# A fused retention and feed-forward kernel: one sum cut in halves, one block prepared earlier, some stores and transposes exchanged

## The chip, the cores and the metric

The kernel runs on one core of one Trainium2 chip. The metric is the device time of one execution in microseconds. Before the change it is 295.54 us, the median of three runs (295.34 to 296.19).

## The reference

Eight batches and eight heads of retention (attention without a softmax, with a decay per head), then two matrix products with `h * cos(h)` between them. All in float32.

```python
def _attn_ref(q, k, v):                       # each (8, 8, 576, 64)
    scores = scale * np.matmul(q, k.transpose(0, 1, 3, 2))      # scale = 1/8
    gamma = 1.0 - 2.0 ** (-5.0 - np.arange(H, dtype=np.float32))
    rel = pos[:, None] - pos[None, :]
    Dmat = np.where(rel >= 0, gamma[:, None, None] ** rel[None, :, :], 0.0)
    return np.matmul(scores * Dmat[None], v)

def _moe_ref(x, w_in, w_out):                 # (4608, 512), (512, 2048), (2048, 512)
    h = x @ w_in
    g = h * np.cos(h)
    return g @ w_out

x = attn_out.transpose(0, 2, 1, 3).reshape(8 * 576, 512)
out = _moe_ref(x, w_in, w_out)                # (4608, 512)
```

## The kernel before

**Tokens.** The 4608 tokens are cut into 18 blocks of 256 (the retention's unit) and 9 tiles of 512 (the two products' unit); tile n holds blocks 2n and 2n+1. The decay is split into a factor on q and one on k, so that a block's retention is: scores of the block with itself under a 0/1 mask, plus q against a state carried from the blocks before, which is a running sum of k times v.

**A block's steps, by function.** `load(j)` brings fq, fk, fv from DRAM, on SP's queue. `scaled` multiplies q or k by its factors and rounds to bf16 (`qks`); `prep(j)` does all four halves of a block on GpSimd. `round_v` rounds v to bf16 (`vb`). The product q·k needs both with the head dimension on partitions: `transpose_dma(j)` does that for a whole block with one transposing transfer on SP's queue (L197, tile `qkT`), `transpose_pe` with eight TensorE instructions and a copy out of PSUM (L210, L215). Blocks 0 to 3 use TensorE, all later ones the transfer. `scores` multiplies (L244 or L282) and puts the mask on with VectorE (`ret`, L262 or L292). `sums_of` multiplies k and v for the state (L319) and adds it to the running one (L349). `out_own` and `out_carried` are the block's two output products (L375, L407), and ScalarE copies the result into `xT`, the first layer's input.

**A tile's steps.** The first layer, `mm1`, works in eight pieces of 1024 columns per partition: TensorE (L445), the cosine on ScalarE (L457), the product with h on VectorE (L460), which writes the bf16 `gT`. The pieces go in turn through the PSUM banks a, b and m. The second layer of tile 0 is a plain product (L927). From tile 1 on, it is done with seven half-size products instead of eight (`mm2_seven`, L563): gT and w_out are cut into quarters, and the products take sums of quarters. The sums of w_out (`ws`) are made once. Those of gT, `gs5`, `gs6`, `gs7` and `gs3`, are made for each tile by `g_sum` (L503): three on VectorE, and one on GpSimd, in four pieces of 128x512. In tile 1 GpSimd makes sum 3, in later tiles sum 7. In tile 1 the products run in the order 1, 2, 4, 6, 5, 7, 3 and in later ones 1, 2, 6, 4, 7, 5, 3. ScalarE copies some products out of PSUM (L593), VectorE adds others to them (L589), and `stored_rows` stores each result in two transfers (L579). The four quarters of a tile's result are c11, c21, c22 and u1; `op` has two buffers for each of the names a, b, c and d.

**What sets the order.** The order on every engine is written by hand; an engine works through its list and waits where a semaphore says so. `at` in the last loop puts the retention of coming blocks between the seven products: `first_scores`, `next_scores` and `last_outputs` in tile 1; `only_intro`, `mid_unit` and `end_unit` in tile 2; `first_unit` and `second_unit` in later ones. `pend` collects the adds and stores of finished products, and `flush` issues them. `sums_after` puts sums behind certain pieces of the first layer, `late_sums` the rest behind the last. `step` is one block's `prep`, `transpose_dma`, `round_v` and the load of a later block; `steps_to` calls it until a block is prepared, and `stored(u)` calls that behind a store. SP's queue carries loads, transposes and stores in one order; the weights come over GpSimd's queue, and some of the last stores over ScalarE's.

**The places of the diff.** At the start, block 1's k has its second transpose on TensorE, and VectorE copies it out (L215) ahead of scaling block 1's q (L167). In tile 1, GpSimd's sum 3 stands between VectorE's sums 6 and 7 in `first_scores` and depends on sum 6 alone; tile 0's stores go out behind the first piece of the first layer, ahead of block 5's transpose; block 7 is prepared behind the store of c22. In tile 2, block 8 is prepared behind the seventh piece of the first layer, and half of VectorE's sum 3 is made behind the sixth. In the last tile, product 5 has three parts, of 256, 128 and 128 columns, for two row halves (the second is cut), of which the two smaller ones share the PSUM tile m; product 3 is accumulated on top of it.

Of the kernel before, what the change touches and what calls it, by code (L numbers as in the profile page):

```python
# [8 lines left out]
F32 = mybir.dt.float32  # L9
# [8 lines left out]
def kernel(  # L18
# [9 lines left out]
    nc = tc.nc  # L28
    P = 128
# [12 lines left out]
    E2 = ET // 2  # L42
# [160 lines left out]
    def transpose_pe(j, name, bank, evac, ys=(0, 1)):  # L203
        if ("qkT", j) not in tiles:
            new_qkT(j)
        m = "qk".index(name)
        ps = psum.tile([P, len(ys), HG, P], BF16, tag=bank, name="tr")
        for u, y in enumerate(ys):
            for hg in range(HG):
                nc.tensor.transpose(  # L210
                    ps[:, u, hg, :],
                    tiles["qks", j][:, m, y, hg].rearrange("s a d -> s (a d)"),
                    ident,
                )
        evac(tiles["qkT", j][:, m, ys[0] : ys[-1] + 1], ps)  # L215
# [298 lines left out]
    def sums_after(n, i):  # L514
        if n == 1:
            slots = {5: ((5, 0, 4),), 6: ((6, 0, 4),)}
        else:
            slots = {
                2: ((7, 0, 4),),
                3: ((5, 0, 4),),  # L520
                4: ((6, 0, 4), (7, 4, 6)),
                5: ((3, 0, 4),),
                6: ((5, 4, 6), (7, 6, E2)),
            }
        for x in slots.get(i, ()):
            g_sum(n, *x)

    def late_sums(n, xs):
        for x in xs:
            g_sum(n, x, 6 if x == 5 and n > 1 else 4, E2)  # L530

    def product(n, x, halfway=None):
        gT = tiles["g", n]
        parts = [(j, 0, N2) for j in range(2)]
        fold = n in (1, last)
        fresh = x not in ((6, 7, 3) if fold else (6, 7))
        if fresh:
            tag = {1: "n", 2: "st", 4: "m" if n == 1 else "st", 5: "st", 3: "n"}[x]
            if x == 5 and n == last:
                ps = psum.tile([P, N2], F32, tag="b", name="o")  # L540
                pt = psum.tile([P, 2, 512], F32, tag="m", name="o")
                tiles["o", x] = [ps] + [pt[:, k, : N2 // 2] for k in range(2)]
            else:
                ps = psum.tile([P, 2, N2], F32, tag=tag, name="o")
                tiles["o", x] = [ps[:, j] for j in range(2)]
                tiles["all", x] = ps
        if x in (5, 3) and n == last:
            parts = [(0, 0, N2), (1, 0, N2 // 2), (1, N2 // 2, N2)]
        dst = tiles["o", x if fresh else 5 if x == 3 else 1]
        lhs = {1: gT[:, :E2, :256], 2: gT[:, E2:, :256], 4: gT[:, E2:, 256:]}.get(x)  # L550
        if lhs is None:
            lhs = tiles["gs", n, x]
        rhs = {1: w_quarter(0, 0), 2: w_quarter(1, 0), 3: w_quarter(1, 1)}.get(x)
        if rhs is None:
            rhs = w_sum[x]
        order = [(e, i) for e in range(E2) for i in range(len(parts))]
        if len(parts) > 2:
            order.sort(key=lambda u: u[1])
        for u, (e, i) in enumerate(order):
            if halfway and u == len(order) // 2:  # L560
                halfway()
            j, c0, c1 = parts[i]
            nc.tensor.matmul(  # L563
                dst[i],
                lhsT=lhs[:, e, j * P : (j + 1) * P],
                rhs=rhs[:, e, c0:c1],
                start=(fresh and e == 0 and (i == 0 or len(parts) > 2)),
                stop=(e == E2 - 1 and (i == len(parts) - 1 or len(parts) > 2)),
                skip_group_check=True,
            )  # L570
        return parts

    def stored_rows(r0, c0, c1, t, queues=(nc.sync, nc.sync)):

        rows = out[r0 : r0 + P * t.shape[1], c0:c1].rearrange(
            "(j i r) c -> r i j c", r=2, i=HP
        )
        for r in range(2):
            queues[r].dma_start(rows[r], t[r * HP : (r + 1) * HP])  # L579

    def mm2_seven(n, at, stored, xs=(1, 2, 6, 4, 7, 5, 3), halfway=None):
# [13 lines left out]

        def store(t, r, c, s):
            def go():
                queues = (nc.sync, nc.scalar) if n == last and s == 2 else (nc.sync, nc.sync)
                stored_rows(n * W + r * 256, c * N2, (c + 1) * N2, t, queues)
                stored(s)  # L600

            return go
# [62 lines left out]
    def load_next(**kw):  # L665
        nonlocal loaded
        if loaded < NB:
            load(loaded, **kw)
            loaded += 1
# [116 lines left out]
    load_next(names="kqv", gate=w_dma[3])  # L786
    ps0 = psum.tile([P, DG, BK], F32, tag="m", name="ov")
    out_own(0, ps0)
    transpose_pe(1, "k", "st", vec, (1,))
    scaled(nc.vector, 1, "q", 0)  # L790
    scaled(nc.vector, 1, "q", 1)
    out_carried(0, ps0)
    act(x_of(0), ps0)
    nc.scalar.activation(sine, half_pi, ACTF.Sin, bias=0.0, scale=1.0)
# [70 lines left out]
    for n in range(NT):  # L865
        blocks = blocks_of.get(n) or [(e + k * E2, 0, W) for e in range(0, E2, 2) for k in range(2)]
        for i, (et, c0, cw) in enumerate(blocks):
            inside = {
                (0, 1): {2: block1_carried},
                (1, 0): {2: lambda: transpose_pe(3, "q", "b", act)},  # L870
                (1, 2): {3: block3_scores},
                (1, 3): {2: lambda: sums_of(3, "st")()()},
            }.get((n, i), {})
            off = [] if (n, i) == (1, 3) else None
            between = block1_sums if (n, i) == (0, 0) else None
            mm1(n, et, c0, cw, banks_of.get(n, "abmabmab")[i], inside, off, between)
            if (n, i) == (0, 0):
                block1_own()
            if (n, i) == (1, 0):
                step(False)  # L880
                load_next()
                for r0, ot in stores:
                    stored_rows(r0, 0, DM, ot)
            if (n, i) == (1, 1):
                step(False)
                load_next()
                step()
            if (n, i) == (1, 3):
                mm2_seven(1, {}, None, (1,), lambda: (outputs(3, "m"), off.pop()()))
            if n:  # L890
                sums_after(n, i)
            if (n, i) == (2, 6):
                step()
        if n == 0:
            gT = tiles["g", n]
            two = psum.tile([P, 2, DM], F32, tag="m", name="o")
# [67 lines left out]

        def first_scores(flush, pend):
            g_sum(n, 5, 4, E2)
            g_sum(n, 6, 4, E2)
            masks = scores(a, "ab")
            add_a = sums_of(a, "st")
            add_b = sums_of(b, "m")  # L970
            masks[0]()
            add_a()()
            masks[1]()
            g_sum(n, 3, 0, E2)
            g_sum(n, 7, 0, 4)
            tiles["rounded"] = add_b()
            g_sum(n, 7, 4, E2)

        def next_scores(flush, pend):
            outputs(a, "a")  # L980
# [30 lines left out]

        def stored(u):
            if n == 1:
                steps_to({2: 8}.get(u, 0))
            else:
                steps_to({0: 2 * n + 6, 3: 2 * n + 7}.get(u, 0))

# [31 lines left out]
```

## Time and profile before

| what | us |
|---|---|
| median of three runs | 295.54 |
| the profiled execution | 296.28 |
| its span, first to last instruction | 294.6 |
| TensorE's matmuls, busy | 283.2 |
| VectorE, busy | 215.6 |
| GpSimd, busy | 145.6 |
| ScalarE, busy | 143.0 |
| tile 1's stage, 51.7 to 86.6: TensorE busy | 33.77 of 34.90 |
| tile 2's stage, 86.6 to 117.5: TensorE busy | 30.57 of 30.90 |
| tile 4's stage, 147.0 to 176.5: TensorE busy | 29.39 of 29.50 |
| the last stage, 264.0 to 294.6: TensorE busy | 25.94 of 30.60 |
| mean granted TensorE clock | 0.994 |

The profiled execution is one execution; its time is compared with its own span, and only then with the median. TensorE's weight loads run beside its matmuls. A busy share says nothing about the order of things: which wait decides is read from the chain of waits and the timelines. Times in a timeline are counted from the span's start. The 16 transfer engines are taken up almost completely until some 215 us (their row over 40 slices shows 9 in all but a few slices), and much less after that.

### The profile page before, as it was taken

To read this page: it belongs to the slowest core of one execution; us is meant where nothing else is said; L and a number is where in the kernel's file an instruction comes from. 1 tells how busy PE (TensorE), PEld (TensorE's weight loads), DVE (VectorE), ACT (ScalarE), POOL (GpSimd) and SP (SyncE) were. 2 spreads that over 40 slices of the span, in tenths; PEclk is the share of its full clock that TensorE was granted. 3 is DMA by queue.
4 is the path that set the end of the run, shared out by engine and by line. 5 is a ranking of instruction groups with operands and counts; after the bars stand their busy time and mean duration, and the time that the engine had idled before them with its cause. 6 is when DMAs were issued, how large, how long until landed. Compare 5 with 4: busy or idle time off the path is not lost.

```text
span 294.6 us, 7623 instructions
## 1 busy us (share of the span) xinstructions
PE 283.2 (96%) x3248; PEld 195.0 (66%) x3268; DVE 215.6 (73%) x268; ACT 143.0 (49%) x166; POOL 145.6 (49%) x172
## 2 busy tenths in 40 slices
PE   7889999999999999999999999999999999999993
PEld 2568755878864688458845884588458845874583
DVE  4585748558986999699659965996599659835933
ACT  4466537646436624563356335633563356326620
POOL 8641535847864495839713961497148014102400
PEclk9799999999999999999999999999999999999999
DMA  7999999999899999999999999979930630121014
GB/s 197 268 222 215 232 247 214 231 181 231 198 199 227 204 240 210 191 219 197 236 203 193 243 215 197 219 128 223 203 64 21 127 71 0 38 65 44 2 37 107
DMA packets 128930, 49.78 MB, mean 169 GB/s; under 512 B 89344, under 2 KB 128384, under 8 KB 128896
## 3 DMA queue, kind: packets, MB, share of 16 engines
q1 hardware_dynamic: 124288, 44.84, 75.6%
q0 software_dynamic: 4224, 4.19, 8.8%
q8 instruction: 25, 0.41, 0.6%
q10 hardware_dynamic: 384, 0.26, 0.4%
q14 instruction: 9, 0.07, 0.1%
HBM read 36.70 MB, written 9.44 MB: 157 GB/s over the span
## 4 chain that ended last, share of the span: by engine, by line
PE 79%; DVE 10%; DMA 4%; POOL 2%; ACT 2%; issue 1%; DVEq 0%; ACTq 0%
PE h L445 38%; PE o L563 27%; PE o L927 5%; DVE gT L460 3%; PE ov L375 3%; DVE gs L503 3%; DMA qkT<-qks 2%; PE st L319 2%; POOL qks L167 2%; PE sc L282 2%; DVE ret L292 2%; PE ov L407 1%; DMA fk<-in_k_dram 1%; PE tr L210 1%; ACT cosh L457 1%
## 5 line engine op out<-in xcount | busy, mean ns | idle before, releaser
L445 PE MATMUL h<-xT,w_in_sb 128*128 128x512 bf16 (+1 forms) x690 | 126.6, 340 | 1.0
L460 DVE TENSOR_TENSOR gT<-h,cosh 128x1024 bf16<-128x1024 f32 x72 | 87.9, 1221 | 37.5 <-ACT cosh L457 37.4
L457 ACT ACTIVATE cosh<-h,half_pi 128x1024 f32<-128x1024 f32 x72 | 80.2, 1114 | 66.4 <-PE h L445 65.1
L445 PEld LDWEIGHTS <-w_in_sb 128*128 128x128 bf16 x704 | 68.4, 98 | 55.3 <-issue 0.6
L503 POOL TENSOR_TENSOR gs<-gT 128x512 bf16<-128x512 bf16 x28 | 35.8, 1280 | 92.2 <-DVE gT L460 92.2
L563 PEld LDWEIGHTS <-gs 128*128 128x128 bf16 x528 | 49.5, 98 | 6.4
L167 POOL TENSOR_TENSOR qks<-fq,gq 128x512 bf16<-128x512 f32 x31 | 33.9, 1113 | 18.1 <-DMA fq<-in_q_dram 14.9
L563 PEld LDWEIGHTS <-gT 128*128 128x128 bf16 x384 | 37.1, 98 | 6.3
L593 ACT COPY ot<-o 128x512 f32<-128x512 f32 x33 | 19.3, 586 | 40.5 <-PE o L563 40.5
L167 POOL TENSOR_TENSOR qks<-fk,gkc 128x512 bf16<-128x512 f32 x28 | 31.8, 1154 | 0.0
L589 DVE TENSOR_TENSOR ot<-ot,o 128x512 f32<-128x512 f32 x35 | 23.2, 680 | 10.9 <-ACT ot L593 7.9
L563 PE MATMUL o<-w_out_sb,gs 128*128 128x256 bf16 (+1 forms) x264 | 30.6, 269 | 0.0
L563 PE MATMUL o<-ws,gs 128*128 128x256 bf16 (+1 forms) x264 | 30.5, 270 | 0.0
L563 PE MATMUL o<-w_out_sb,gT 128*128 128x256 bf16 x256 | 30.5, 273 | 0.0
L292 DVE TENSOR_TENSOR ret<-sc,mask_c 128x1024 bf16<-128x1024 f32 x25 | 29.7, 1214 | 0.1
L430 ACT CAST xT<-ov 128x1024 bf16<-128x1024 f32 x16 | 16.2, 1013 | 11.0 <-PE ov L407 11.0
L178 POOL CAST vb<-fv 128x512 bf16<-128x512 f32 x31 | 18.7, 624 | 5.7 <-DMA fv<-in_v_dram 5.6
L503 DVE TENSOR_TENSOR gs<-gs,gT 128x1024 bf16<-128x1024 bf16 x16 | 15.7, 982 | 0.3
L503 DVE TENSOR_TENSOR gs<-gT 128x512 bf16<-128x512 bf16 (+1 forms) x25 | 15.4, 615 | 0.4
L563 PE MATMUL o<-ws,gT 128*128 128x256 bf16 x128 | 15.3, 273 | 0.0
L349 DVE TENSOR_TENSOR s<-st,s 128x256 f32<-128x256 f32 x18 | 7.6, 421 | 10.4 <-PE st L319 10.1
L359 ACT CAST sb<-s 128x512 bf16<-128x512 f32 (+1 forms) x18 | 10.3, 573 | 9.3 <-DVE s L347 3.8
(81 smaller groups left out, 203.4 us busy)
## 6 DMA issues: line engine op xcount, KB each, us to landing
out_dram<-ot SPq DMA_DIRECT2D x69, 128.0 KB, 2.6
fk<-in_k_dram SPq DMA_DIRECT2D x25, 256.0 KB, 5.7
fv<-in_v_dram SPq DMA_DIRECT2D x25, 256.0 KB, 5.1
fq<-in_q_dram SPq DMA_DIRECT2D x12, 512.0 KB, 5.3
w_in_sb<-in_moe_w_in_dram POOLq DMA_DIRECT2D x4, 512.0 KB, 8.1
w_out_sb<-in_moe_w_out_dram POOLq DMA_DIRECT2D x4, 512.0 KB, 9.8
fk<-in_k_dram SPq DMA_DIRECT2D x3, 512.0 KB, 5.3
fv<-in_v_dram SPq DMA_DIRECT2D x3, 512.0 KB, 7.0
```

The lines of the kernel that those rows point to most:

```text
L167: return eng.tensor_tensor(out=dst.rearrange("p b a d -> p a b d"), in0=src.rearrange("p (a b) d -> p a b d", a=2), in1=by.rearrange("p (a ...
L178: runs[y](vb[:, y], f[:, :, y, :] if j < NP_B else f[:, y])
L292: nc.vector.tensor_tensor(out=ret[:, k].rearrange("p a b i -> p (a b) i"), in0=pss[k].rearrange("p a b i -> p (a b) i"), in1=mask.unsqueez ...
L430: evac(x, ps)
L445: nc.tensor.matmul(ps[:, j, :], lhsT=w_in_sb[:, dg, (et + j) * P : (et + j + 1) * P], rhs=xT[:, dg, c0 : c0 + w], start=(dg == 0), stop=(d ...
L457: nc.scalar.activation(cosh, ps, ACTF.Sin, bias=half_pi, scale=1.0)
L460: nc.vector.tensor_mul(gT[:, et : et + m, c0 : c0 + w], ps, cosh)
L503: i = eng.tensor_tensor(out=tiles["gs", n, x][:, e : e + step], in0=a[:, e : e + step], in1=b[:, e : e + step], op=op_,)
L563: nc.tensor.matmul(dst[i], lhsT=lhs[:, e, j * P : (j + 1) * P], rhs=rhs[:, e, c0:c1], start=(fresh and e == 0 and (i == 0 or len(parts) > 2)),
L589: return lambda: nc.vector.tensor_tensor(out=out_, in0=in0, in1=in1, op=ALU.add)
L593: nc.scalar.copy(t, tiles["all", x])
L927: nc.tensor.matmul(pss[t], lhsT=gT[:, e, t * P : (t + 1) * P], rhs=w_out_sb[:, e, :], start=(e == 0), stop=(e == ET - 1),)
```

## The change

1. At the start, VectorE scales block 1's q before it copies block 1's second k transpose out of PSUM.
2. In tile 1, GpSimd's sum 3 is made in two halves. The first waits for VectorE's sum 6, the second stands behind sum 7 and waits for it.
3. Tile 0's stores go behind block 5's transpose on SP's queue, and the one of buffer d goes first of them.
4. Block 7 is prepared behind tile 1's last store instead of behind that of c22, without a load. So the stores of c11 and u1 go ahead of its transpose.
5. In tile 2, block 8's q is scaled on GpSimd behind the third piece of the first layer, and its k behind the fifth. Behind the seventh come its transpose, its v, and the loads of blocks 9 and 10.
6. In tile 2, VectorE's sum 3 is made whole, behind the masks of `only_intro`, instead of in two halves.
7. In the last tile, the three parts of product 5 have three PSUM tiles (b, m and a), and the second half of c21's store goes to ScalarE's queue.

TensorE's instructions and their order stay the same.

```diff
@@ sums_after, late_sums
-                5: ((3, 0, 4),),
+                5: ((3, 0, 4),) if n > 2 else (),
...
-            g_sum(n, x, 6 if x == 5 and n > 1 else 4, E2)
+            g_sum(n, x, 6 if x == 5 and n > 1 else 0 if x == 3 and n == 2 else 4, E2)
@@ product
-                ps = psum.tile([P, N2], F32, tag="b", name="o")
-                pt = psum.tile([P, 2, 512], F32, tag="m", name="o")
-                tiles["o", x] = [ps] + [pt[:, k, : N2 // 2] for k in range(2)]
+                tiles["o", x] = [
+                    psum.tile([P, c], F32, tag=t, name="o")
+                    for t, c in (("b", N2), ("m", N2 // 2), ("a", N2 // 2))
+                ]
@@ store
-                queues = (nc.sync, nc.scalar) if n == last and s == 2 else (nc.sync, nc.sync)
+                queues = (nc.sync, nc.scalar) if n == last and s else (nc.sync, nc.sync)
@@ start
-    transpose_pe(1, "k", "st", vec, (1,))
     scaled(nc.vector, 1, "q", 0)
     scaled(nc.vector, 1, "q", 1)
+    transpose_pe(1, "k", "st", vec, (1,))
@@ the loop over the first layer's pieces
             if (n, i) == (1, 0):
                 step(False)
                 load_next()
-                for r0, ot in stores:
-                    stored_rows(r0, 0, DM, ot)
             if (n, i) == (1, 1):
                 step(False)
+                for r0, ot in stores[3:] + stores[:3]:
+                    stored_rows(r0, 0, DM, ot)
                 load_next()
                 step()
...
+            if n == 2 and i in (2, 4):
+                for y in range(2):
+                    scaled(nc.gpsimd, 8, "q" if i == 2 else "k", y)
             if (n, i) == (2, 6):
-                step()
+                transpose_dma(8)
+                round_v(8)
+                prepared = 9
+                load_next()
+                load_next()
@@ first_scores
-            g_sum(n, 6, 4, E2)
+            six = g_sum(n, 6, 4, E2)
...
-            g_sum(n, 3, 0, E2)
+            g_sum(n, 3, 0, 4, gate=six)
             g_sum(n, 7, 0, 4)
             tiles["rounded"] = add_b()
-            g_sum(n, 7, 4, E2)
+            seven = g_sum(n, 7, 4, E2)
+            g_sum(n, 3, 4, E2, gate=seven)
@@ stored
             if n == 1:
-                steps_to({2: 8}.get(u, 0))
+                if u == 3:
+                    step(False)
```

## The prediction

> **What bounds the kernel now.** I read the busy shares first, then the chain of waits in order of time, then the timeline of single engines around the places that the diff touches. The shares:
>
> ```profile
> PE 283.2 (96%) x3248; PEld 195.0 (66%) x3268; DVE 215.6 (73%) x268; ACT 143.0 (49%) x166; POOL 145.6 (49%) x172
> ...
> POOL gs L503 <- DVE gT L460: 92.2, 27, 17.0
> ```
>
> TensorE has work nearly all the time, so only time in which it stands can be won: 294.6 - 283.2 = 11.4 us, most of it in the first 18 us, in the tail after the last matmul (290.1 to 294.6), and around 80 us. The second line, of the waits, shows that GpSimd's long waits are for its own inputs: it has room. The steady tiles give the scale: from 147.05 to 176.49 us one takes 29.44 us with no recorded wait. The places of the diff, in the timeline (start, duration, engine, line, operation, out and in):
>
> ```profile
> 14.05 0.40 PE L210 MATMUL tr<-ident,qks 128*128 128x128 bf16 x4
> ...
> 14.49 0.43 DVE L215 COPY qkT<-tr 128x512 bf16<-128x512 bf16 x1 [1.37 <-PE tr L210]
> ...
> 14.83 1.28 DVE L167 TENSOR_TENSOR qks<-fq,gq 128x512 bf16<-128x512 f32 x2
> ...
> 15.57 0.40 PE L210 MATMUL tr<-ident,qks 128*128 128x128 bf16 x4 [0.56 <-DVE qks L167]
> ...
> 17.08 0.64 PE L244 MATMUL sc<-qkT 64*64 64x128 bf16 x32
> ```
>
> The reader is to see VectorE idle for 1.37 us before the copy of k, and the scaling of q behind it; TensorE then waits for q.
>
> ```profile
> 74.50 5.44 POOL L503 TENSOR_TENSOR gs<-gT,gs 128x512 bf16<-128x512 bf16 x4
> ...
> 75.16 1.53 DVE L503 TENSOR_TENSOR gs<-gs,gT 128x1024 bf16<-128x1024 bf16 x1
> ...
> 78.88 1.60 DVE L503 TENSOR_TENSOR gs<-gT 128x1024 bf16<-128x1024 bf16 x1
> ...
> 81.19 0.68 DVE L503 TENSOR_TENSOR gs<-gT 128x1024 bf16<-128x1024 bf16 x1
> ...
> 81.33 0.42 PE L282 MATMUL sc<-qkT 64*64 64x128 bf16 x16 [0.38 <-DVE s L349]
> ...
> 84.19 0.41 PE L375 MATMUL ov<-ret,vb 128*64 128x128 bf16 x8 [0.25 <-DVE ret L292]
> ```
>
> The same VectorE sum takes 0.68 us alone and 1.53 or 1.60 beside GpSimd's sum; in this stretch the chain of waits runs through VectorE, and TensorE stands twice.
>
> ```profile
> 68.96 5.81 SPq L579 DMA_DIRECT2D out_dram<-ot  x8
> ...
> 74.88 2.27 SPq L197 DMA_TRANSPOSE qkT<-qks  x1
> ...
> 93.85 3.14 SPq L579 DMA_DIRECT2D out_dram<-ot  x4
> ...
> 97.59 2.27 SPq L197 DMA_TRANSPOSE qkT<-qks  x1
> ...
> 108.92 3.10 SPq L197 DMA_TRANSPOSE qkT<-qks  x1
> ...
> 115.19 0.64 PE L282 MATMUL sc<-qkT 64*64 64x128 bf16 x32 [0.22 <-DMA qkT<-qks]
> ```
>
> SP's queue issues without a pause here; each transpose has stores ahead of it. Those at 74.88, 97.59 and 108.92 are blocks 5, 7 and 8. A transpose lands 4.4/5.1/6.9 us (least, median, most) after its issue starts; block 8's is late by 0.22 us.
>
> **The change part by part.**
>
> *Start: block 1's q ahead of the copy.* VectorE's masks end at 13.12. The two fq loads issued by then landed 5.5 and 7.3 us after issue, the second was issued at 4.97, so it is there by 12.27. The scaling (1.21 us by the chain) runs 13.13 to 14.36, and the copy of k still starts at 14.49, when its transpose is out: nothing is queued behind a new wait. TensorE's own order is the same. Its first q transposes follow the idle matmul, at 15.05 instead of 15.57 (15.57 less the 0.56 wait, plus the start); the second four follow 0.22 later. From transpose start to copy start is 0.46 (15.57 to 16.03), a copy is 0.42: copies 15.51 to 15.93 and to 16.35; the scores start at 16.41 instead of 17.08, so -0.67. What follows has to keep up: xT is written by 15.75, block 1's v is rounded at 18.2 and its sums come at 19.51 - 0.67 = 18.84. Then everything rests on TensorE until block 2's transposes at 38.4, whose k is scaled at 35.1. Bounds: 0 if any of these slips, -0.9 if the second copy also hides (16.17 to 15.27).
>
> *Tile one: GpSimd's sum in halves.* Sum 3 now waits for VectorE's sum 6, and its second half for sum 7. Sum 6 keeps 0.68 (-0.85). GpSimd's first two pieces, at 1.28 each by the group's mean, lie beside the masks, 75.9 to 78.4; the masks ran at 1.21 beside it before too. Sum 7's first half then waits about 0.2 for it and ends near 78.95 instead of 80.48; the state sums (0.87) end at 79.8, before TensorE gets to the second half of the scores, about 80.83: the 0.38 goes. Masks end 83.3 instead of 84.13; TensorE, after product 7 (1.75 us) at 82.93, waits about 0.17 there. Adding up from 80.83: scores 0.35, product 1.75, output 0.25 + 0.17 + 0.34, carried 0.35, product 3 1.76, so tile two starts at 85.8 instead of 86.64: -0.84. The second half of sum 3 (2.56 from 80.45) ends at 83.0, and product 3 asks for it after 84.9. GpSimd's next work waited for its load until 83.83, so this is covered. Bounds: -0.4 (only sum 6 is cured) and -1.15 (TensorE without a gap from 75.04, 10.4 us).
>
> *Block 5's transpose ahead of tile zero's stores.* It starts at 68.96 and lands by 75.9 at the most. Its scores start at 80.55 before, and near 79.9 with the start's gain: left where it was it would land at 79.98 (74.88 + 5.1), or 81.8 at worst, and be the next wait. So it is worth 0 by itself and carries the two gains above. The stores move back 2.27 us; only buffer d is needed again soon, by the copy at 79.96, and its stores are put first, landing near 71.2 + 1.5 + 2.6 = 75.3.
>
> *Blocks 7 and 8, loads 9 and 10.* Stores of c11 and u1 go ahead of transpose 7, load 9 behind transpose 8. With the rows' durations: stores 93.85 to 100.55 (3.14 + 3.56), transpose 7 to 102.8, landing by 107.5 at most; scores of block 7 at 111.35, with the gains about 109.8. Transpose 8 starts at 102.8 instead of 108.92, its q and k being scaled inside layer one, and lands by 109.7; needed near 113.7. The 0.22 goes. Loads 9 and 10 then fill 106 to 117.3, so by the next store (118.12 before) SP is where it was. GpSimd starts block 9 near 112 instead of 108.51, and has it near 118, before its transpose at 120.95: covered by the stores ahead of it.
>
> *Tile two's first layer.* Four GpSimd instructions of 1.03 to 1.25 us go between its sums, beside VectorE, which is back to back from 94.89 to 103. VectorE loses the 0.68 of sum 3 there (99.63) and pays 1.3 of it after the masks at 108.98, ahead of an idle 0.71: it ends by 110.3, wanted at 115.8. Collisions are visible:
>
> ```profile
> 103.06 1.02 DVE L503 TENSOR_TENSOR gs<-gT 128x512 bf16<-128x512 bf16 x1
> 104.11 1.42 DVE L503 TENSOR_TENSOR gs<-gs,gT 128x1024 bf16<-128x1024 bf16 x1
> ```
>
> These are 0.42 and 0.68 alone, and both end about 0.5 behind the end of a GpSimd instruction: a VectorE sum waits out what GpSimd runs. Laid out, sum 5 loses 0.36, the later piece of sum 5 about 0.55, less the 0.68: the last gT ends at 103.55 instead of 103.03, and product 2 wants it at 102.2 + 12 x 0.109 = 103.5. I take +0.1; bounds 0 and +1.9 (below).
>
> By the Trainium skill, SBUF — State Buffer, section "Who interferes with whom", a VectorE instruction with two SBUF inputs contends with a GpSimd instruction that reads SBUF, and the loser is blocked for the whole of it. The trace agrees as far as the two rows above go; taken at its full length for each sum it is the second rival.
>
> *Tail.* Product 5's and 3's third part get a bank of their own, so the add of part two need not wait for part three: only one add (0.29) follows the last matmul instead of two (0.49 together), -0.2. The second half of c21's store moves from SP to ACT's queue: SP's last issue goes from 291.22 to about 290.95. The two overlap; I take -0.25, bounds 0 and -0.6 (one issue).
>
> Sum: -0.67 - 0.84 - 0.22 + 0.1 - 0.25 = -1.88. The profiled execution took 296.28 (294.6 span, 1.68 around it), so 294.4 by it; it was 0.74 above the median of 295.54, and I carry the difference to the median: 293.7.
>
> **Rivals.**
>
> 1. *The transfers catch TensorE.* SP's queue runs without a pause to 146 us and does not move earlier, so an advance of 1.5 us eats its lead. Block 10's transpose at 133.87 lands at 139 (5.1) or 140.8 (6.9); its scores go from 142.84 to about 141. Against it: no recorded wait for a transfer after 115 us. If half the advance is lost: 294.5.
>
> 2. *GpSimd holds VectorE in tile two.* If three sums there wait a whole 1.03 each, 3.1 less 0.68, the last gT is 2.4 late, at 105.4, and product 2 stands 1.9 us: 295.5. For it: the rows 1.02 and 1.42. Against: GpSimd's pieces are gated by gT, so most starts fall behind VectorE's.
>
> 3. *Slower: transpose 7 behind eight stores.* Place: SP from 93.85. The slowest stores by rows took 1.36 each (2.72 for two at 118.12): eight are 10.9, transpose 7 starts at 104.7 and lands by 111.6, 1.8 after 109.8, which only gives back the gain. It decides from a landing later than 111.7 on, one for one; the stretched stores and a transpose 8 queued behind it could make it 113: 296.8. Against: the same eight took 6.7 in the trace.
>
> 4. *It does not do what it says.* Sum 3's first half still meets sum 7 at full length (1.60), and the start's gain ends at the copies: -0.3 - 0.4 - 0.2 = -0.9: 294.6.
>
> **How the numbers follow.** Forecast 0.55, rival one 0.12, two 0.10, three 0.10, four 0.13. The forecast's own range is 293.0 to 294.4. A measurement of this kernel tells about 0.3% (0.89 us) from no change, so faster means below 294.65: the forecast, rival one and half of rival four, and none of two: 0.74. Same: rival two and half of four, 0.16. Slower, above 296.4: rival three, 0.10. The range holds 8 in 10: from 292.9, a little past the forecast's low end, to 295.3, which leaves out most of rivals two and three.
>
> **What would show it.** Right: scores of block 1 near 16.4; VectorE's sum 6 of tile one at 0.7 and sum 7's first half under 1; tile two's first matmul near 85.1; no wait for a transpose near 114; one add behind the last matmul. Wrong: a wait in front of block 7's scores; product 2 of tile two starting late or with gaps; TensorE waiting in tile three for a transpose; tile zero's first matmul still at 17.66.

## The result, and the profile after

| | before | after |
|---|---|---|
| median (14 runs each, taken in turn) | 295.67 us (295.33 to 298.26) | 294.79 us (293.93 to 296.26) |
| ratio of after to before | | 0.9957, 95% interval 0.9937 to 0.9977 |
| the profiled execution | 296.28 us | 294.94 us |
| its span | 294.6 us | 293.2 us |

The changed kernel is faster, by 0.2 to 0.6 per cent; timed once more later it stood at 0.9943 (0.9919 to 0.9967). The ratio in the table is that of the two means (294.76 to 296.02 us); the medians alone give 0.9970. The forecast of 293.7 us was too low by 1.1, and the result lies within the range of 292.9 to 295.3. The prediction drew its line for "faster" at 294.65, and the median stands 0.14 above it, so by its own line this is the edge of "same". The shares first (first row of the changed kernel's page):

```profile
PE 284.1 (97%) x3268; PEld 194.8 (66%) x3268; DVE 215.6 (74%) x267; ACT 142.9 (49%) x166; POOL 145.5 (50%) x172
```

TensorE's busy time is not less (284.1, with more of its records in the trace); what has shrunk is the time in which it stands. Next the places of the diff, in the timelines of the changed kernel (start, duration, engine, line, operation, out and in; in brackets the idle time just before, and what ended it). The start:

```profile
13.23 1.28 DVE L167 TENSOR_TENSOR qks<-fq,gq 128x512 bf16<-128x512 f32 x2
14.69 0.42 DVE L215 COPY qkT<-tr 128x512 bf16<-128x512 bf16 x1 [0.17 <-PE tr L210]
15.68 0.76 DVE L215 COPY qkT<-tr 128x512 bf16<-128x512 bf16 x2 [0.57 <-PE tr L210]
...
16.49 0.64 PE L244 MATMUL sc<-qkT 64*64 64x128 bf16 x32 [0.19 <-DVE qkT L215]
```

The scaling has filled VectorE's idle time ahead of the copy, and block 1's scores stand at 16.49 instead of 17.08. Tile one:

```profile
76.27 2.27 POOL L503 TENSOR_TENSOR gs<-gT,gs 128x512 bf16<-128x512 bf16 x2 [0.69 <-DVE gs L503]
...
75.14 0.98 DVE L503 TENSOR_TENSOR gs<-gs,gT 128x1024 bf16<-128x1024 bf16 x1
...
78.31 0.78 DVE L503 TENSOR_TENSOR gs<-gT 128x1024 bf16<-128x1024 bf16 x1
...
79.97 0.62 PE L282 MATMUL sc<-qkT 64*64 64x128 bf16 x32
```

The two VectorE sums take 0.98 and 0.78 us, not 1.53 and 1.60. The scores of block 5 are one group of 32 without a wait, where they were two of 16 with a wait between. Tile two's first matmul follows at 85.27. SP's queue:

```profile
68.68 4.65 SPq L197 DMA_TRANSPOSE qkT<-qks  x1
73.42 5.03 SPq L580 DMA_DIRECT2D out_dram<-ot  x8
...
84.77 4.80 SPq L197 DMA_TRANSPOSE qkT<-qks  x1
...
101.73 5.78 SPq L197 DMA_TRANSPOSE qkT<-qks  x2
...
113.00 2.26 SPq L135 DMA_DIRECT2D fq<-in_q_dram  x1
...
121.04 1.70 SPq L580 DMA_DIRECT2D out_dram<-ot  x2
```

In the kernel before, block 6's transpose, load 10 and the first store of tile two were these:

```profile
84.42 3.26 SPq L197 DMA_TRANSPOSE qkT<-qks  x1
...
112.07 0.59 SPq L135 DMA_DIRECT2D fq<-in_q_dram  x1
...
118.12 2.72 SPq L579 DMA_DIRECT2D out_dram<-ot  x2
```

Block 5's transpose, which now stands behind loads instead of stores, takes 4.65 us of the queue instead of 2.27, and block 6's, behind loads in both kernels, 4.80 instead of 3.26. Block 5's k was scaled by 61.25 and block 6's by 71.78, so neither waits for its input. The load of block 10 goes out at 113.00 (112.07 before, though TensorE is now 1.5 us ahead), and the first store of tile two, which was to be back in its place at 117.3, goes out at 121.04 (118.12 before). Who notices is read from tile three, GpSimd's rows first:

```profile
123.71 1.26 POOL L178 CAST vb<-fv 128x512 bf16<-128x512 f32 x2
124.93 2.72 POOL L503 TENSOR_TENSOR gs<-gT 128x512 bf16<-128x512 bf16 x2
...
125.53 1.11 DVE L503 TENSOR_TENSOR gs<-gT 128x1024 bf16<-128x1024 bf16 x1
...
129.82 2.08 PE L564 MATMUL o<-w_out_sb,gT 128*128 128x256 bf16 x16
```

The first quarter of sum 7, sum 5 and product 1 in the kernel before:

```profile
122.71 1.15 POOL L503 TENSOR_TENSOR gs<-gT 128x512 bf16<-128x512 bf16 x1
...
127.03 0.69 DVE L503 TENSOR_TENSOR gs<-gT 128x1024 bf16<-128x1024 bf16 x1
...
131.33 1.91 PE L563 MATMUL o<-w_out_sb,gT 128*128 128x256 bf16 x16
```

Block 10 is rounded on GpSimd until 124.97, so GpSimd's sum 7 begins 2.2 us later than before (122.71) and lies beside VectorE's sum 5, which takes 1.11 instead of 0.69. Product 1 takes 2.08 instead of 1.91. Taken step by step from the starts of TensorE's groups in the two profiles:

| stretch | before, us | after, us | difference | forecast |
|---|---|---|---|---|
| to the first product with w_in behind block 1's scores | 17.66 | 17.07 | -0.59 | -0.67 |
| from there to tile two's first matmul | 68.98 | 68.20 | -0.78 | -0.84 |
| to the state's product behind product 2 of tile two | 17.40 | 17.54 | +0.14 | +0.1 |
| to tile three's first matmul | 13.48 | 13.20 | -0.28 | -0.22 |
| tile three | 29.37 | 29.69 | +0.32 | 0 |
| from tile four's first matmul to the end of the last add | 143.68 | 143.47 | -0.21 | -0.25 |
| sum | | | -1.40 | -1.88 |

Five of the six stretches are within 0.1 us of the forecast, and the sixth was not in it. These are two executions. Over all executions the difference is -0.88 us by the medians and -1.26 by the means in this comparison, and -1.80 and -1.71 in the later one.

### The profile page after: what moved, and what is told of

Read it like the earlier page. It is cut to its first block, busy times and chain, and to the rows that moved or that the text cites. A ratio compares the mean times of both kernels' runs of the same rounds, so it can differ in the third digit from the quotient of the medians.

```text
span 293.2 us, 7643 instructions
## 1 busy us (share of the span) xinstructions
PE 284.1 (97%) x3268; PEld 194.8 (66%) x3268; DVE 215.6 (74%) x267; ACT 142.9 (49%) x166; POOL 145.5 (50%) x172
## 4 chain that ended last, share of the span: by engine, by line
PE 93%; DVE 2%; DMA 1%; ACT 1%; issue 0%; DVEq 0%; ACTq 0%
PE h L445 42%; PE o L564 34%; PE o L935 5%; PE ov L375 3%; PE st L319 2%; PE sc L282 2%; PE ov L407 2%; DMA fk<-in_k_dram 1%; PE tr L210 1%; DVE ret L262 1%; PE sc L244 1%; DVE qks L167 0%; PE idle L220 0%; DVE gT L460 0%; DVE ret L255 0%
## 5 line engine op out<-in xcount | busy, mean ns | idle before, releaser
L167 POOL TENSOR_TENSOR qks<-fk,gkc 128x512 bf16<-128x512 f32 x28 | 31.0, 1122 | 1.1 <-DMA fk<-in_k_dram 1.0
L178 POOL CAST vb<-fv 128x512 bf16<-128x512 f32 x31 | 19.3, 637 | 6.1 <-DMA fv<-in_v_dram 5.8
L503 DVE TENSOR_TENSOR gs<-gT 128x512 bf16<-128x512 bf16 (+1 forms) x25 | 16.5, 661 | 0.4
L935 PE MATMUL o<-w_out_sb,gT 128*128 128x512 bf16 x64 | 15.0, 380 | 0.0
L503 DVE TENSOR_TENSOR gs<-gs,gT 128x1024 bf16<-128x1024 bf16 x16 | 14.7, 920 | 0.3
```

The lines of the kernel that those rows point to most:

```text
L167: return eng.tensor_tensor(out=dst.rearrange("p b a d -> p a b d"), in0=src.rearrange("p (a b) d -> p a b d", a=2), in1=by.rearrange("p (a ...
L178: runs[y](vb[:, y], f[:, :, y, :] if j < NP_B else f[:, y])
L503: i = eng.tensor_tensor(out=tiles["gs", n, x][:, e : e + step], in0=a[:, e : e + step], in1=b[:, e : e + step], op=op_,)
L935: nc.tensor.matmul(pss[t], lhsT=gT[:, e, t * P : (t + 1) * P], rhs=w_out_sb[:, e, :], start=(e == 0), stop=(e == ET - 1),)
```

## The experiments

Each kernel was timed in turn with the kernel before, so its ratio counts; the medians of the kernel before in the later three comparisons were 296.34, 296.71 and 296.84 us. All diffs are against the changed kernel except the first.

**The start alone.** The kernel before, with nothing but the new order at the start.

```diff
+    scaled(nc.vector, 1, "q", 0)
+    scaled(nc.vector, 1, "q", 1)
     transpose_pe(1, "k", "st", vec, (1,))
-    scaled(nc.vector, 1, "q", 0)
-    scaled(nc.vector, 1, "q", 1)
```

> The kernel before with the start's edit alone (block 1's q scaled ahead of the copy). My theory: block 1's scores start about 0.6 us earlier (near 16.5) and everything on TensorE moves with them, until block 5's scores: block 5's transpose still goes out behind tile 0's stores, near 74.9, and lands near 80, while the scores are wanted near 79.9, so 0 to 0.6 us is lost again there. Tile two's first matmul between 86.0 and 86.6, the time 0.0 to 0.6 us under the kernel before. Rival (the parts add up independently): the whole 0.6 us arrives, tile two starts at 86.0, no wait for a transpose in tile one.

Measured: 296.62 us, ratio 1.0011 (0.9987 to 1.0036). Block 1's scores come at 15.56 and block 4's at 73.95, 1.1 earlier than before, of which a part is not the edit's: this execution began at full clock, the one before at half (table below). Tile two starts at 86.88, 0.24 later than before, so theory and rival both missed, and nothing waits for block 5's transpose. The timeline of tile one tells where it goes:

```profile
74.91 5.25 POOL L503 TENSOR_TENSOR gs<-gT,gs 128x512 bf16<-128x512 bf16 x4
...
76.98 2.79 PE L563 MATMUL o<-ws,gs 128*128 128x256 bf16 x24 [0.78 <-DVE gs L503]
...
81.56 0.42 PE L282 MATMUL sc<-qkT 64*64 64x128 bf16 x16 [0.69 <-DVE s L349]
```

GpSimd's sum 3 begins when block 6's v has been rounded (74.83), not when TensorE is ready; it is at 74.91 here and was at 74.50. TensorE arrives earlier and waits longer for the VectorE work beside it. Without the halves the start shows no gain.

**The halves taken back.** GpSimd's sum 3 in one piece, ungated.

```diff
-            g_sum(n, 3, 0, 4, gate=six)
+            g_sum(n, 3, 0, E2)
...
-            g_sum(n, 3, 4, E2, gate=seven)
```

> The changed kernel with GpSimd's sum 3 in one piece behind sum 6, as before. My theory: GpSimd's sum begins when block 6's v has come, near 74.5, whatever TensorE does; VectorE's sums 6 and 7 take 1.5 and 1.6 us again, and tile two begins near 86.6 to 86.9, as in the kernel with the start alone, so the start's gain is lost too; the end is 1.2 to 1.6 us later than in the changed kernel. Rival (the collisions cost only what the waits say, 0.6 to 0.8 us): tile two at 86.0 to 86.1.

Measured: 295.67, ratio 0.9971 (0.9946 to 0.9996). In its timeline of VectorE and TensorE:

```profile
75.72 1.52 DVE L503 TENSOR_TENSOR gs<-gs,gT 128x1024 bf16<-128x1024 bf16 x1
...
79.44 1.60 DVE L503 TENSOR_TENSOR gs<-gT 128x1024 bf16<-128x1024 bf16 x1
...
81.89 0.42 PE L282 MATMUL sc<-qkT 64*64 64x128 bf16 x16 [0.76 <-DVE s L349]
```

Both sums are long again, and tile two starts at 87.20 instead of 85.27. The halves are worth 1.9 us at that point, more than the 0.84 of the sum, since they also let the start's gain through. Of these, tile three gives 0.3 back: it takes 29.37 here. By the ratios, 0.9971 here against 0.9957 and 0.9943 of the changed kernel, the halves are worth 0.4 to 0.8 us in the end, less than the 1.2 to 1.6 expected.

**The start taken back, twice.** The changed kernel with the old order at the start; the second time beside the changed kernel itself.

```diff
+    transpose_pe(1, "k", "st", vec, (1,))
     scaled(nc.vector, 1, "q", 0)
     scaled(nc.vector, 1, "q", 1)
-    transpose_pe(1, "k", "st", vec, (1,))
```

> The changed kernel with the start's order as before. My theory: with the halves in place VectorE no longer pins tile one to GpSimd's loads, so the start's gain shows where it is taken out: block 1's scores 0.6 us later after the first masks, and tile two's first matmul and the end 0.4 to 0.7 us later than in the changed kernel. Rival (something fixed by transfers absorbs the start): tile two at 85.3 as in the changed kernel.

> The changed kernel with the order at the start as before, timed once more beside the changed kernel itself. Theory (the start's gain of 0.6 us in the profile is partly taken back, because block 2's and 3's work then waits for transfers that have not moved): 0 to 0.3 us above the changed kernel. Rival (the start is worth its 0.6 us in the median too): 0.5 to 0.7 us above.

> The changed kernel unaltered, timed beside the variants: 0.3 to 0.6 per cent below the kernel before; TensorE's first matmul of tile two near 85.2 us, tile three 29.6 to 29.8 us.

Measured: 294.91, ratio 0.9939 (0.9919 to 0.9960); again 295.09, 0.9942 (0.9920 to 0.9965), beside 295.04, 0.9943 (0.9919 to 0.9967), of the changed kernel. So the start's edit shows 0.05 us in the median. That is nearer to the theory's 0 to 0.3 than to the rival's 0.5 to 0.7, but each ratio is uncertain by 0.2 per cent, some 0.7 us, so the times alone do not exclude the rival. Tile two starts at 85.01 and 85.75 without the edit and at 85.27 and 85.19 with it; the first expectation, 0.4 to 0.7 us later, holds for the second of these profiles and not for the first. The profiles show why 0.6 us of gain in a trace need not be in a median. They fall in two kinds by TensorE's granted clock from 9 to 11 us, 0.50 or 1.00, which no edit here touches:

| clock at 9 to 11 us | kernel | block 0's first mask | block 1's scores | block 3's scores |
|---|---|---|---|---|
| 0.50 | before; start taken back (again) | 10.76; 10.65 | 17.08; 16.98 | 57.01; 56.90 |
| 0.50 | after; gated sum 7; stores held (below) | 10.96; 10.85; 10.86 | 16.49; 16.39; 16.40 | 56.42; 56.32; 56.33 |
| 1.00 | start taken back; with gated sum 7 (below) | 9.90; 10.06 | 16.23; 16.39 | 56.16; 56.31 |
| 1.00 | after (again); stores split (below) | 10.11; 10.12 | 15.64; 15.66 | 56.08; 56.67 |
| 1.00 | block 5's transpose, blocks 7 and 8 taken back (below) | 10.02; 10.13 | 15.55; 15.68 | 55.92; 56.70 |
| 1.00 | start alone; halves taken back; block 5's transpose (again) | 10.03; 10.10; 10.30 | 15.56; 15.64; 15.84 | 55.91; 56.00; 55.88 |

From block 0's first mask to block 1's scores the old order takes 6.32 to 6.33 us and the new one 5.53 to 5.55, at either clock. In the executions that begin at half the clock the gain is still there at block 3. In the seven that begin at full clock with the new order, block 3's scores come 0.1 to 0.4 earlier than in the two with the old one in five, and 0.4 to 0.5 later in the other two. What takes the gain back was read in one of these two. There, with the stores split, TensorE waits for block 3:

```profile
51.33 1.03 PE L445 MATMUL h<-xT,w_in_sb 128*128 128x256 bf16 x8 [0.49 <-ACT xT L430]
```

By ScalarE's timeline that is for block 3's v, which is cast from 48.74 on, when its load has landed.

**Block 5's transpose.** Tile zero's stores back ahead of it.

```diff
             if (n, i) == (1, 0):
                 step(False)
                 load_next()
+                for r0, ot in stores:
+                    stored_rows(r0, 0, DM, ot)
             if (n, i) == (1, 1):
                 step(False)
-                for r0, ot in stores[3:] + stores[:3]:
-                    stored_rows(r0, 0, DM, ot)
```

> The changed kernel, with tile 0's stores back ahead of block 5's transpose. My theory: the transpose goes out near 74.5 and lands 79.5 to 81.5; block 5's scores, at 79.97 in the changed kernel, wait 0.3 to 1.5 us for it, TensorE shows that wait, and tile two starts at 85.6 to 86.6 instead of 85.27; the time is 0.3 to 1.2 us above the changed kernel's (ratio to before 0.997 to 1.000). Rival (the transpose had room where it was): tile two at 85.3 and the changed kernel's time, ratio near 0.9957.

Measured: 296.04, ratio 0.9996 (0.9963 to 1.0028). The profiled execution took 294.27: transpose at 74.67, a wait for it of only 0.26 us (TensorE's weight loads for block 5's scores, at 79.73), tile two at 85.07, and tile three at 29.37. But the twelve times have two groups, seven from 293.98 to 296.04 and five from 297.57 to 299.18; the median says nothing of either. So the same kernel was profiled once more:

> The changed kernel with tile 0's stores back ahead of block 5's transpose, once more, for another profile: its executions spread from 293.98 to 299.18 us. My theory: in the long ones the transpose lands after block 5's scores want it (near 79.9) and TensorE stands there, 1 us or more. Rival: the long ones lose their time elsewhere (block 8's transpose, or the start).

That execution took 297.97. Its queue and TensorE timelines:

```profile
70.20 6.44 SPq L580 DMA_DIRECT2D out_dram<-ot  x8
76.74 3.20 SPq L197 DMA_TRANSPOSE qkT<-qks  x1
...
82.05 0.97 PE L282 MATMUL sc<-qkT 64*64 64x128 bf16 x32 [2.45 <-DMA qkT<-qks]
82.95 3.20 PE L564 MATMUL o<-w_out_sb,gs 128*128 128x256 bf16 x16
```

The stores begin 1.9 us later than in the other execution, the transpose lands too late, and TensorE stands for 2.45 us. What follows is slow as well: 0.97 for scores that take 0.62 to 0.64, 3.20 for a product of 1.92. The windows of the same execution show the clock (stretch, its length, busy time and instructions of PE, PEld, DVE, ACT and POOL, the granted clock, the transfers' share and GB/s):

```profile
74.00:79.50 5.50, 5.50 (x112) 4.63 (x112) 5.46 (x6) 1.95 (x4) 4.40 (x5) 1.00 1.09 174
79.50:82.05 2.55, 0.10 (x9) 0.00 (x1) 1.03 (x3) 1.71 (x3) 1.41 (x2) 1.00 0.82 181
82.05:86.10 4.05, 4.05 (x50) 2.88 (x50) 2.36 (x2) 0.30 (x1) 1.73 (x2) 0.58 1.13 252
```

A wait of 2.45 us brought 4.05 us at 0.58 of the clock. Tile two starts at 88.76 against 85.07 in the first profile of the same kernel: 3.7 us for a wait of 2.45. In the forecast this step had the price 0 "by itself", with the wait named as the next one; in some executions the wait is there.

**Half of the stores ahead.** Four of tile zero's eight transfers go before block 5's transpose.

```diff
             if (n, i) == (1, 1):
+                for r0, ot in stores[3:] + stores[:1]:
+                    stored_rows(r0, 0, DM, ot)
                 step(False)
-                for r0, ot in stores[3:] + stores[:3]:
+                for r0, ot in stores[1:3]:
```

> The changed kernel with block 5's transpose behind four of tile 0's eight stores instead of ahead of all. My theory: a transpose right behind loads takes long on SP's queue (4.65 us in the changed kernel, 2.1 to 2.3 us behind stores) and slows the transfers; here it takes under 3.5 us, load 10 goes out 1 to 2.5 us earlier than in the changed kernel (113.0), GpSimd's sum 7 starts by 123.5, tile three takes 29.4 instead of 29.7; the transpose lands by 77. Time 0.3 us below the changed kernel's. Rival: SP is as late as in the changed kernel and tile three takes 29.7.

Measured: 294.49, ratio 0.9939 (0.9913 to 0.9965). The transpose takes 1.57 (at 73.51), under 3.5 as expected, but the queue is no earlier afterwards: block 6's transpose is at 85.01 and load 10 at 112.74. Tile three takes 30.27, with VectorE's sum 5 at 1.70. No gain over the changed kernel can be told from these times.

**Blocks 7 and 8 taken back.** Block 7 prepared behind the store of c22, block 8 behind the seventh piece, loads 9 and 10 and VectorE's sum 3 of tile two as before.

```diff
-                5: ((3, 0, 4),) if n > 2 else (),
+                5: ((3, 0, 4),),
...
-            g_sum(n, x, 6 if x == 5 and n > 1 else 0 if x == 3 and n == 2 else 4, E2)
+            g_sum(n, x, 6 if x == 5 and n > 1 else 4, E2)
...
-            if n == 2 and i in (2, 4):
-                for y in range(2):
-                    scaled(nc.gpsimd, 8, "q" if i == 2 else "k", y)
             if (n, i) == (2, 6):
-                transpose_dma(8)
-                round_v(8)
-                prepared = 9
-                load_next()
-                load_next()
+                step()
...
-                if u == 3:
-                    step(False)
+                steps_to({2: 8}.get(u, 0))
```

> The changed kernel, with blocks 7 and 8, loads 9 and 10 and VectorE's sum 3 of tile two as before. My theory: tile two loses no time at product 2 (3.59 us for products 1 and 2 instead of 3.73) and tile three takes 29.4 us from first matmul to first matmul instead of 29.7, but block 8's transpose goes out near 109 and lands 113.5 to 115.5, while its scores are wanted at 113.4, so TensorE stands 0.3 to 1.8 us there. Time between the changed kernel's and 1.2 us above it. Rival (this part is a net loss): no such wait, and 0.3 to 0.5 us below the changed kernel.

Measured: 298.98, ratio 1.0077 (1.0050 to 1.0104), the slowest of all. Its queue and TensorE timelines:

```profile
111.32 3.14 SPq L197 DMA_TRANSPOSE qkT<-qks  x1
...
116.24 1.07 PE L282 MATMUL sc<-qkT 64*64 64x128 bf16 x32 [2.30 <-DMA qkT<-qks]
117.24 2.80 PE L564 MATMUL o<-w_out_sb,gs 128*128 128x256 bf16 x16
```

Block 8's transpose goes out 2.4 us later than before (108.92) while TensorE comes 1 us earlier, so the wait of 0.22 is one of 2.30, followed by 3.56 us at a clock of 0.60 (columns as above):

```profile
116.24:119.80 3.56, 3.56 (x48) 2.79 (x49) 2.35 (x2) 0.00 (x0) 0.88 (x1) 0.60 1.13 260
```

Products 1 and 2 of tile two take 3.59 and tile three 29.37, both as expected; but by the ratios the time is 3.6 to 4.0 us above the changed kernel's, where 1.2 at most was expected. This part of the change is not worth 0.22: without it the other parts would make the kernel slower than it was.

**Tile one's stores held.** They go behind block 8's transpose, and load 9 directly behind block 7's.

```diff
+    held = []
+
...
-                stored_rows(n * W + r * 256, c * N2, (c + 1) * N2, t, queues)
+                if n == 1:
+                    held.append((n * W + r * 256, c * N2, (c + 1) * N2, t))
+                else:
+                    stored_rows(n * W + r * 256, c * N2, (c + 1) * N2, t, queues)
...
-                load_next()
+                for s in held:
+                    stored_rows(*s)
                 load_next()
...
-                    step(False)
+                    step()
```

> The changed kernel, with tile 1's eight stores held back behind block 8's transpose, and load 9 again right behind block 7's transpose. My theory: the loss in tile three (29.69 us from first matmul to first matmul against 29.37 before) comes from load 10 being late, which makes GpSimd's sum 7 late and has it meet VectorE's sum 5. Here load 10 goes out near 110 instead of 113, GpSimd's sum 7 starts near 121 to 122 instead of 124.9, VectorE's sum 5 takes 0.7 us instead of 1.11, tile three takes 29.4; the time is 0.3 us below the changed kernel's, ratio to before near 0.9945. Rival (TensorE, being 1.5 us earlier, meets GpSimd whatever the loads do): tile three keeps 29.7 and the time is the changed kernel's.

Measured: 295.21, ratio 0.9963 (0.9939 to 0.9987). The expectation missed: load 10 goes out later, at 114.61, because the eight stores now stand ahead of it; VectorE's sum 5 takes 1.18, and tile three 29.76. It neither helps nor tells the theories apart.

**Sum 7 of tile three gated.** Each of its quarters waits for the VectorE sum just ahead of it.

```diff
+        if n == 3:
+            slots = {
+                3: ((5, 0, 4), (7, 0, 2)),
+                4: ((6, 0, 4), (7, 2, 4)),
+                5: ((3, 0, 4), (7, 4, 6)),
+                6: ((5, 4, 6), (7, 6, E2)),
+            }
+        done = None
...
-            g_sum(n, *x)
+            done = g_sum(n, *x, gate=done if n == 3 else None)
```

> In tile three, each quarter of GpSimd's sum 7 waits for a VectorE sum that stands just ahead of it. Theory (tile three takes 29.69 us in the changed kernel instead of 29.37, because block 10's late load pushes GpSimd's sum 7 to 124.9 us, where it meets VectorE's sum 5, which then takes 1.1 us instead of 0.7): load 10 still goes out near 113 us and block 10 is still prepared late, but no VectorE sum of tile three's first layer takes over 0.75 us, and tile three takes 29.35 to 29.45 us; the span is about 0.3 us below the changed kernel's. Rival (the lateness reaches TensorE by another way, a late transpose or late masks): tile three stays at 29.6 to 29.8 us although the sums are short.

> Both edits together: sum 7 of tile three gated, the start's order as before. If tile three's loss is what the change gave back, and the start pays nothing, this is 0.3 us below the changed kernel, with tile three at 29.4 us; if the start pays its 0.6 us, it is 0.3 us above.

Measured: 294.82, ratio 0.9926 (0.9898 to 0.9954), 0.22 below the changed kernel beside it, which its interval cannot tell from none; with the old start besides, 295.21, 0.9952 (0.9926 to 0.9977), 0.17 above it and no clearer. The expectation of tile three missed: it takes 29.71, as the rival said. VectorE's and TensorE's timelines of the first:

```profile
125.64 0.69 DVE L503 TENSOR_TENSOR gs<-gT 128x1024 bf16<-128x1024 bf16 x1
...
127.38 0.80 DVE L503 TENSOR_TENSOR gs<-gs,gT 128x1024 bf16<-128x1024 bf16 x1
...
133.33 0.67 DVE L503 TENSOR_TENSOR gs<-gT 128x512 bf16<-128x512 bf16 x1
...
136.51 0.67 DVE L598 TENSOR_TENSOR ot<-ot,o 128x512 f32<-128x512 f32 x1
...
129.94 1.91 PE L572 MATMUL o<-w_out_sb,gT 128*128 128x256 bf16 x16
...
137.23 1.91 PE L572 MATMUL o<-ws,gT 128*128 128x256 bf16 x16
```

Half of the theory stands: without the first collision sum 5 takes 0.69 and product 1 its 1.91. But the pieces of sum 7 now end later, the other sums lose 0.05 to 0.26 each, and TensorE waits elsewhere. Product 4 follows the end of a VectorE add, by 0.05 us here (137.18), by 0.05 in the changed kernel (137.05 to 137.10) and by 0.09 in the one before (138.20 to 138.29). Counted from tile three's first matmul, that add ends at 20.68 before, 21.04 after and 21.06 here. VectorE's work from the last gT of the tile to that add has almost no pause. In the changed kernel sum 5 loses 0.42 us, and the last gT ends 16.69 us behind the tile's first matmul instead of 16.39; so most of what VectorE loses in the layer shows in the tile.

The version with the old start ran with load 10 at 116.67, the latest of all, in a long execution (297.42), and shows the same at its worst:

```profile
126.11 1.28 DVE L503 TENSOR_TENSOR gs<-gT 128x1024 bf16<-128x1024 bf16 x1
...
128.45 1.63 DVE L503 TENSOR_TENSOR gs<-gs,gT 128x1024 bf16<-128x1024 bf16 x1
...
133.05 0.61 PE L572 MATMUL o<-w_out_sb,gT 128*128 128x256 bf16 x4 [1.16 <-DVE gT L460]
...
144.10 0.64 PE L282 MATMUL sc<-qkT 64*64 64x128 bf16 x32 [0.26 <-DMA qkT<-qks]
```

Here GpSimd is still scaling and rounding block 10 (124.80 to 128.41) beside the first of the two sums; the second, from 128.45 on, meets the first quarter of GpSimd's sum 7 (128.38 to 129.53). Block 10's transpose is late too.

**All profiles together.** How far load 10's issue lies ahead of tile three's first matmul, and what tile three takes:

| kernel | lead of load 10, us | tile three, us |
|---|---|---|
| halves taken back | 6.38 | 29.37 |
| block 5's transpose taken back (again; first) | 5.94; 5.19 | 29.37; 29.37 |
| start alone | 5.76 | 29.37 |
| before | 5.45 | 29.37 |
| blocks 7 and 8 taken back | 5.36 | 29.37 |
| stores split | 3.38 | 30.27 |
| after (again; first) | 3.26; 3.01 | 29.73; 29.69 |
| start taken back (first; again) | 3.23; 2.93 | 30.44; 30.30 |
| gated sum 7 | 2.63 | 29.71 |
| stores held | 1.22 | 29.76 |
| gated sum 7, old start | -0.07 | 31.58 |

With a lead over 5 us tile three always takes 29.37; with 3.4 and less it takes 0.3 to 2.2 more. These are all fourteen profiles, of eleven kernels. None has a lead between 3.38 and 5.19, so where the loss begins is not known. The amount depends on which instructions meet, and it is not the amount of a median: both profiles with the start taken back, for one, are the longest of their kernel's timed executions (295.30 and 295.95).

The first profile with block 5's transpose taken back answers the rival of the held stores, that TensorE meets GpSimd because it is early, whatever the loads do:

```profile
110.48 1.15 SPq L135 DMA_DIRECT2D fq<-in_q_dram  x1
...
122.86 2.27 POOL L503 TENSOR_TENSOR gs<-gT 128x512 bf16<-128x512 bf16 x2
...
125.18 0.69 DVE L503 TENSOR_TENSOR gs<-gT 128x1024 bf16<-128x1024 bf16 x1
```

TensorE begins tile three at 115.67 there, earlier than in the changed kernel (116.01). But load 10 goes out 2.5 us earlier, sum 7 begins 2.1 us earlier, sum 5 keeps its 0.69, and the tile takes 29.37. So the loss goes with the late load and not with the early TensorE. These two kernels differ only in the place of block 5's transpose; but in the second profile of the same kernel load 10 goes out at 113.42, so that place alone does not set it.

## Why the prediction was right, and where it was not

The sign and the order of size were right; the forecast's own range, 293.0 to 294.4, was missed by 0.4 us, and the result is nearest to the prices of rivals one and four.

*The start, -0.67.* Right in the profile (-0.59), by the steps named; the changed execution reached block 0's first mask 0.2 us later (10.96 against 10.76), so from there on the gain is 0.79. In the median it shows 0.05, with the uncertainty said above. For executions that begin at full clock the bound "0 if any of these slips" was nearer in some cases: in the one that was read, TensorE waits for block 3's v, which comes with its load and was not among the things that the forecast went through. The forecast took one execution's start for all.

*Tile one, -0.84.* Right: -0.78, sums at 0.98 and 0.78 in place of 1.53 and 1.60, no wait between block 5's scores. Sum 6 was to keep 0.68; it still ran beside GpSimd's rounding of block 6 (74.63 to 75.58). Taking the halves back costs 1.9 us at tile two's start, because the start's gain hangs on them.

*Block 5's transpose, 0 by itself.* Right in what it prevents: a wait of 2.45 us, and 3.7 us of time, in the one long execution that was profiled. Wrong in its price on the queue: "The stores move back 2.27 us" took the duration from a row with stores ahead of it, and behind loads the same transpose took 4.65. Over all profiles it took 2.80 to 4.67 us behind loads (nine of them) and 1.57 to 3.20 behind stores (five).

*Blocks 7 and 8, -0.22.* The wait of 0.22 went, as said, and the stretch gained 0.28. But the part was priced against the queue of the kernel before. Against the queue that the other parts leave, it is what keeps a wait of 2.30 us away.

*Loads 9 and 10, 0: the step that failed.* "Loads 9 and 10 then fill 106 to 117.3, so by the next store (118.12 before) SP is where it was", and what GpSimd does behind load 10 was not followed at all. The store went out at 121.04, not 117.3, and load 10 at 113.00. Of these 3.7 us, 1.5 were there when tile one's stores began (95.30, where the sum kept the 93.85 of before), and 2.2 came in the two loads (13.5 us from 107.56 on, where the sum had 11.3). Block 9 was covered. Block 10 was not: GpSimd's sum 7 stands behind it in the same list, and it was moved beside VectorE's sums. That cost 0.32 us in the profile and 0.3 to 1.1 in other executions of kernels with the same queue order. This is rival one's mechanism, transfers that do not move as TensorE does, by a path that the rival did not name: it looked for a wait ahead of block 10's scores, which appeared only with the old start (0.26 to 0.39 us in three profiles).

*Tile two's first layer, +0.1.* Right (+0.14): two sums collide there (1.26 and 1.12 us), and not the three whole ones of rival two. The reading under it, that two sums end "about 0.5" behind a GpSimd instruction, holds for the second row (0.55) and less for the first (0.28, behind 103.80).

*Tail, -0.25.* -0.20 from the one add in place of two. From the end of the last add to the end of the span it is 4.03 us in both kernels, so the store on ScalarE's queue shows no gain. The two halves of this part were not tried apart.

*From the profile to the median.* The forecast took the sum over one execution for the change of the median. The profiles differ by 1.40 us, the medians by 0.88 in one comparison and 1.80 in the other; why these two differ so much stays open.

Rival three did not come: block 7's and 8's transposes went out at 101.73 to 107.51 and nobody waited for them. Rival four's price was near, but its mechanism was not there: the first half of sum 3 does not hold up sum 7 (0.78), and the start's gain does not end at the copies.

Not settled: whether a version that keeps load 10 early and block 5's transpose first would have the missing 0.3 us. The best ratio, 0.9926 with the gated sum, does not stand apart from the changed kernel's.

## What to carry to other kernels

Price a moved transfer by a row with the same neighbours on its queue, and follow the queue until it is really back in its place; then look at every instruction behind the one that the late load feeds, not only at who reads it. Parts of one change depend on each other: a part can look worth 0.2 us against the kernel before and be worth over 2 against the other parts. And where times of one kernel fall in two groups, profile once more: the first profile may be of the group that shows nothing.

## What the runs showed of the hardware

- After a wait of 2.45 or 2.30 us TensorE's granted clock stood at 0.58 and 0.60 over the next 4.05 and 3.56 us, and the first of these waits made tile two start 3.7 us later, half as much again as the wait itself; after 1.16 us (old start with gated sum 7) it stayed at 1.00. The Trainium skill, TensorE: Matmul & The Clock Gate, section "What's actually happening", has the drop after at least one idle window of about 3.4 us; here less than that was enough.
- From 9 to 11 us the clock is 0.50 in some executions and 1.00 in others of the same kernel (the changed one: 0.50 in its first profile, and the first mask at 10.96 against 10.11 in the other). That is 0.85 us at block 0. The Trainium skill says in the same section of that page that the moment of the change varies from run to run.
- One transpose took between 1.57 us (stores split, behind four stores) and 4.80 us (after, behind loads) of SP's queue, with its input ready in both. What sets it is not known.
